# A new order for all five queues of a fused attention and gated-MLP layer

## The chip, the core and the metric

One Trainium2 chip, one of its cores. The metric is the device time of one execution in microseconds (us). Each of the core's five engines works through its own queue in order: PE (matrix products), ACT (activations), DVE (vector work), POOL (vector work) and SP (which here only issues transfers). They meet through semaphores. All transfers run on 16 shared DMA engines.

## The reference

One layer over 2048 positions of width 448, with a modulation computed from a condition vector `c`. A is attention with 16 heads of width 28 and a causal window of 256 positions; B is a gated MLP whose gate mixes positions with a full 2048 x 2048 matrix.

```python
mod = silu(c) @ w_mod                 # six vectors: sa, ca, ga, sb, cb, gb
h = layernorm(x) * (1 + ca) + sa
x = x + ga * A(h, wqkv, wo)           # attention, window 256
h = layernorm(x) * (1 + cb) + sb
x = x + gb * B(h, w_in, w_sp, b_sp, w_out)
# B: z = gelu(h @ w_in); z1, z2 = halves of z; g = w_sp @ layernorm(z2) + b_sp; (z1 * g) @ w_out
```

## The kernel before

The positions are cut into 16 tiles of 128, in four groups of four. Everything stays in the core's own memory between the stages.

- **Loads.** `x_sb` is loaded as tiles 0-1, 2-3, 4-7, 8-11 and 12-15. `w_mod` comes as `wmodA` (the first two vectors, in four pieces, two issued by SP and two by ACT) and `wmodB` (the other four vectors, 1568 KB in one transfer on SP). `wq_st` holds the K and the Q columns of `wqkv` (two pieces each, one on SP and one on ACT), `wv` the V columns. `w_in` comes in three chunks of 448 KB and two halves of 224 KB.
- **First layernorm.** DVE takes the statistics of a tile (L628, L630), POOL the power for the reciprocal root (L632), DVE or POOL writes the normalized tile to `xn` (L643, L650, with L648 for its offset). Group 0 is transposed on PE (L739) and scaled with `modT` on the way out (L748, L750). The other groups are transposed by transfers that SP issues (L465), and then scaled in place (L731). `modT` comes from PE products of `wmodA` (L545) or `wmodB` (L535, with a copied piece `wmodE`, L582); the gates `gg_sb` from L593 and L596.
- **Q, K, V.** L796 makes Q of the first group tile by tile, L762 the Q of later groups, L820 K tile by tile, L840 V.
- **Attention.** For each tile scores (L925 for the first two tiles, L955 and L966 for the rest), exponentials (L911 on ACT), masks (L995, L974 on DVE), products with V (L1002), division (L1016, L1018), a transpose by SP, the output projection (L1028), the residual (L1032) and the second layernorm.
- **The MLP.** L1122 and L1143 make the two halves of z, L1167 mixes positions (28 groups of 16 matmuls, four 512-position blocks `tb` times seven `ft`), L1171 and L1174 form the gated product, L1186 the output product, L1196 the residual. The mixing matrix comes in as 32 transposing transfers, 16 to `wspA` (blocks 0 and 1) and 16 to `wspB` (blocks 2 and 3).

No planner runs in the kernel. The program is a list of numbered operations, and a string `PLAN` says in which order they go out: each word is an engine's letter (p PE, a ACT, d DVE, t POOL, s SP), the operation's number, and after dots the buffer slots that it takes. `Sched.order()` appends the operations to the engines' queues in that order, `count()` and `waits()` work out the semaphore waits from the dependences, and `emit()` writes them out. An operation that several engines can do goes to the engine named by the letter. A word's place in the string matters only against words of the same engine and against users of the same slots.

Numbers that are used below: s14, s1, s10, s12, s13 load x tiles 12-15, 0-1, 2-3, 4-7, 8-11; s20 and s21 the halves of `w_in`'s last chunk, s17 to s19 its other chunks; s2 and s4 `wmodA`; s6 and s8 the K and Q columns; s11 `wv`; s15 `wmodB`; s16 `wo_g`; s193 to s196 are the transposes of x tiles 4 to 7. d186 normalizes tile 4. p45 to p48 are the products of `wmodA`, p125 and p128 the first PE transposes, p93 to p97 the gate products.

Of the kernel before, what the change touches and what calls it, by code (L numbers as in the profile page):

```python
# [22 lines left out]
a403 a43 p421.0 a422.6.0 t249 t253 d404 t251 t199 p375 p379 p381 d406 d382 d399 t252.2 d163 p217.0 p218 a219
a169 p210.1 p211 d212 p429.0 a430.0 p201.0 p202 a203 d168 p204.1 p205 a206 s14 d309 d383.2 p398.0 p400 p448.0
a449.2.1 s16 d426 s831 s258 t254.1 s259 d250.0 d255 d425 d432 d311 s384 s257 t256.3 s260 t100 t99 t261 t102
t262 t264 p226.0 p423.0 a424 p207.1 p227 p405 p208 d228 d305 p407 d408 d409.1 d306 s410 d101 d310 d431 a209
d215 d453 p456.0 p229.0 a457.1 d459 d214 d458 d452 p220.1 p221 p230 a231 p427.0 p428 s833 p475.0 p433 p434
d435 p223.0 p224 d225 d312 p450.0 a222 p232.1 d436.2 s437 d213 a476.3.2 d480 p483.0 d307 p233 d234 p235.0 p236
a451 a216 p477.0 p454.0 p455 a484.0 p501.0 d485 d486 d308 s21 s17 s834 p460 p461 d462 d479 d463.0 s464 a237
t263 p385.0 p386 d387 p411.1 p412 a478 p503.0 d413 t313 a502.6.0 p528.0 a504 d388 d505 d389 p481.0 p482 p487  # L30
p488 p271.0 p530.0 d489 d490.1 a529.2.1 d533 d506 d532 p272 a273 p509.0 a510.5 p268.1 p274.0 p275 d276 p269
d270 p507.0 p508 a531 p555.0 a556.3.2 p281.0 p265.1 p266 a267 d512 p282 p557.0 a558 a283 d511 p513 t317 t318.1
s323 t319 t320.2 s324 d314.0 s321 t315 t316.3 s322 t328 d279 d414 d560 p536.0 a537.1 p438.1 p439 d440 d280
p514 d515 d516.0 p287.0 p288 a289 p290.1 p291 a292 p563.0 a564.5 p238.0 p239 d278 p293.1 p534.0 p294 p535
p582.0 a240 p465.0 p466 d441 d442 d538 d415 d277 s20 s491 s830 s517 t390 d539 d391.2 t392 s393 a295 a583.4.0
d559 p540 p541 p284.1 p584.0 p285 a286 p590.0 a591.2 d566 d467 p299.0 p300 a301 d542 d543.1 p561.0 p562 d586
d565 d468 p567 p568 p608.0 t416 t327 t325 d326 d587 p518.1 p335.0 p519 d569 d570.0 p588.0 a585 p589 p336 d593
d469 d520 a609.3.1 p616.0 d592 d521 d417 d522 t523 t470 t418.0 t524 p338.1 p339 a337 s544 p545.0 p546 s18 p594
p595 a617.5 p635.0 a636.6.2 p610.0 a611 d340 p492.1 p493 d547 p296.0 p297 a298 t471 d596 d597.2 d612 p614.0
d613 s835 s571 s598 d494 t419 s420 d640 d548 d619 d549 d618 d495 t443 t444 t445.1 t446 s447 p662.0 a663.0.0  # L40
d667 p615 p332.0 p333 a334 p329.1 p330 a331 d639 d343 t472.2 d473 s474 p643.0 a644.1 p599.0 p600 p637.0 a638
p345.1 p346 p620 a347 d601 d602 d344 d645 d666 d342 p670.0 a671.2 p621 p664.0 d622 d496 p348.0 p349 a350
p357.1 p358 t550 t551 t552.0 t804 d623.2 s624 p689.0 d646 d673 d525.2 p302.0 p303 d304 d672 s19 p641.0 p642
p647 p648 d649 d805 t553 d650.0 s651 t526 s527 t497 t806 t803 d498.1 t499 s500 a690.5.1 p697.0 a359 p351.1
p352 d341 d353 a665 d693 d603 a698.1 d700 d694 p668.0 p363.0 p364 a365 p715.0 a716.3.2 p669 p674 p675 p691.0
a692 d699 d676 d677.2 s678 p354.1 p355 p572.0 a356 d720 d719 p723.0 a724.2 p717.0 a718 p573 d574 d575 p695.0
p696 p701 d725 p702 d703 d704.0 s705 s554 d576 p652.0 p742.0 a743.0.1 p366.1 p367 a368 d726 p653 d654 t577
d578 t579.2 d746 d655 p721.0 p722 p727 p750.0 a751.4 p728 d747 d729 d730.1 s731 p360.1 p361 p625.0 p744.0 p626
p769.0 d752 d627 d753 d628 a362 p748.0 p679.1 p680 d681 a745 p749 p754 p755 d756 d757.2 p771.0 a770.6.0 p777.0
a772 p706.1 p707 p732.0 p733 d773 d774 p775.0 p776 t580 s581 t809 a778.1 p852.0 p853.1 p854 d656 d708 d734  # L50
d779 d682 d780 d808 t604 d605.0 s758 p759.0 p760 d761 p781 p782 d783 d784.0 a856 d629 t630 t631 p855 a862
p868.3 p869.2 p870 p871 a878 a872 p980.0 p981.1 p982 p983 a986 a987 d735 d736 t657 t658 t606 t659.2 d857 d683
t810 t807 p884.3 p885.2 p886 p887 d709 d710 d632.1 d762 d763 d879 d633 s369 s825 s785 s826 s607 t684 d685 s634
a984 a985 p900.0 p901.1 p902 p903 t737 t711 t660 d686.0 t687 a894 d895 d896 t764 a888 p996.3 p997.2 p998 p999
s661 d712.1 d858 d738 s688 s840 s824 s823 a904 p988.0 d905 a814 a910 p989.1 p990 a1000 a1001 a1003 a992 a1002
a993 p786.0 t799 t797 t713 t811 t813 t801 t812 d765 d889 t766.0 d859 d863 d874 d906 s714 d864 t767 s768 d907
t739.2 d897 d912 t898 d865 d880 d890 p787 d788 d740 s741 s832 p991 a995 d789 d790 t791 d873 d911 d875 t792
d793.1 p932.2 a994 p933.0 p934 p935 a936 d937 p916.1 p917.3 a942 d944 d938 d943 d913 p918 a920 d922 p919 a926
p1004.0 p1005.1 p1006 p1007 a1011 a1009 a1010 a1008 t860 t794 s795 t818 d817 t816 d891 d815 d881 d939 d927
d899 d928 d945 t914 t876 d877 d921 t908 d909 t882 d923 p948.2 p949.3 p950 p951 p964.1 p965.0 p966 a952 d929  # L60
d953 d954 a958 d959 d955 d883 d960 t892 t956 d893 t940 p967 a968 a974 p1028.3 p1029.1 p1030 p1031 t866 t930
t946 t924 t800 a1032 a1033 p1012.2 p1013.3 p1014 a1034 p1020.0 a1035 p1021.1 p1022 p1015 a1017 a1016 a1018
# [5 lines left out]
d1079.0 t1080 t1092 p1045.4 p1039.6 d1046.1 p1153.1 t798 t1047 d1040.0 t1041 d1139.0 p1075.6 p1114.2 p1054.4
p1141.0 p1150.7 d1055.1 t1056 d1076.1 p1060.4 p1147.6 t1077 p1096.5 t1140 d1154.0 p1144.1 d1061.3 d1115.1
p1093.2 d1097.0 t1155 d1145.0 p1102.3 p1063.1 p1057.4 t1146 d1142.0 s1098 d1103.0 t1116 p1105.5 s1062 d1151.1  # L70
d1094.3 t1152 d1058.2 s1059 d1148.1 t1149 d1106.1 t1107 p1069.4 d1070.1 s1071 d1064.1 s1095 s1065 p1108.7
p1117.5 p1111.0 d1109.1 t1110 d1112.1 t1143 p1167.2 p1066.1 t1113 p1163.4 d1118.0 t1119 s1104 d1067.0 s1068
p1168 d1169.0 s1170 p1171.0 p1172 d1173.2 s1174 p1126.3 p1129.6 d1130.0 d1127.1 s1128 s1131 p1159.5 p1160
p1164 d1161.3 s1162 p1099.2 d1165.0 d1100.2 s1101 s1166 p1132.5 d1133.3 s1134 p1135.3 d1136.1 s1137
# [1194 lines left out]
```

## Time and profile before

| | |
|---|---|
| runs | 277.11, 276.43, 281.8 us; median 277.11 |
| the profiled execution | 277.96 us, of which the profile's span is 276.2 us |
| what lies around the span | 1.76 us |
| busy share of the span | PE 97%, PE weight loads 56%, DVE 59%, ACT 44%, POOL 43% |
| chain that ended last, by engine | PE 78%, DVE 13%, DMA 4% |

A line of the chain or of the timeline has its start, its duration, the engine, the tile written and the line of the kernel. "x16" is a count of instructions. A line of a group gives its total busy time and the mean of one in nanoseconds, then the idle time ahead of it and what ended it. A line of the waits gives who waited for whom, the total, the times and the longest. A line of transfers gives the size of one and the median time from issue to landing.

### The profile page before, as it was taken

How to read it: one execution, taken by the hardware profiler on the slowest of the kernel's cores; microseconds unless marked ns; L12 is line 12 of the kernel's file. 1: busy time of each engine (PE TensorE's matmuls, PEld its weight loads, DVE VectorE, ACT ScalarE, POOL GpSimd, SP SyncE). 2: the span in 40 equal slices, each digit the busy share in tenths (PEclk: the TensorE clock that was granted, in tenths of full speed). 3: DMA queues.
4: the chain of work that ended last, by engine and by line, in shares of the span. 5: the costliest groups of instructions: out<-in, count | busy, mean ns of one | idle time of the engine just before them, and what ended most of it. 6: DMA issues, size and time to landing. Idle time of an engine off the chain costs nothing.

```text
span 276.2 us, 8403 instructions
## 1 busy us (share of the span) xinstructions
PE 268.5 (97%) x3751; PEld 155.1 (56%) x3751; DVE 163.7 (59%) x365; ACT 121.5 (44%) x142; POOL 118.1 (43%) x160
## 2 busy tenths in 40 slices
PE   7999998999999899999999999999999999999995
PEld 5976686678677676544444444444444444454552
DVE  3799999979899989939789301221212022153143
ACT  2599998899899689476766500000000000000000
POOL 7565467626574231498258003254453023062320
PEclk9999999999999799999999999999999999999999
DMA  7999744845442533658499996000000000001013
GB/s 206 316 221 189 96 101 114 107 96 110 114 63 61 107 60 61 176 114 141 97 155 191 213 182 135 0 0 0 2 0 0 0 2 0 33 17 63 0 39 116
DMA packets 67301, 25.54 MB, mean 92 GB/s; under 512 B 58497, under 2 KB 66178, under 8 KB 67266
## 3 DMA queue, kind: packets, MB, share of 16 engines
q1 hardware_dynamic: 66304, 24.21, 43.8%
q10 hardware_dynamic: 962, 0.80, 1.1%
q8 instruction: 29, 0.48, 0.8%
q14 instruction: 6, 0.05, 0.1%
HBM read 9.01 MB, written 1.84 MB: 39 GB/s over the span
## 4 chain that ended last, share of the span: by engine, by line
PE 78%; DVE 13%; DMA 4%; POOL 1%; SPq 1%; issue 1%; DVEq 0%
PE ps L1167 35%; PE ps L1122 8%; PE ps L1143 8%; PE ps L1186 8%; PE ps L1002 5%; DVE PT L974 4%; PE ps L1028 4%; PE ps L955 3%; DMA x_sb<-in_A_x_dram 3%; PE ps L820 3%; PE ps L762 2%; DVE st_all L628 2%; PE ps L840 2%; DMA hT<-xn 2%; DVE o_sb L1018 1%
## 5 line engine op out<-in xcount | busy, mean ns | idle before, releaser
L1174 POOL TENSOR_TENSOR z1T<-tmpg,z1T 128x512 bf16<-128x512 bf16 x28 | 32.0, 1153 | 77.2 <-DVE tmpg L1171 77.2
L1171 DVE TENSOR_TENSOR tmpg<-ps,bsp_bc 128x512 bf16<-128x512 f32 x28 | 19.0, 689 | 76.0 <-PE ps L1167 64.7
L911 ACT ACTIVATE PW<-ps 128x2048 bf16<-128x2048 f32 (+1 forms) x42 | 59.9, 1451 | 6.1 <-PE ps L955 4.5
L1167 PE MATMUL ps<-wspB,z 128*128 128x512 bf16 x224 | 50.1, 379 | 0.0
L1167 PE MATMUL ps<-wspA,z 128*128 128x512 bf16 x224 | 49.5, 379 | 0.0
L632 POOL TENSOR_TENSOR rs_all<-mv_all,neghalf 128x1 f32<-128x1 f32 (+2 forms) x37 | 24.1, 672 | 34.3 <-DVE mv_all L630 34.3
L974 DVE TENSOR_TENSOR PT<-PW,mask 128x1024 bf16<-128x1024 bf16 x56 | 38.0, 702 | 0.2
L1167 PEld LDWEIGHTS ps<-wspA,z 128*128 128x128 bf16 x224 | 21.8, 98 | 26.6 <-issue 0.4
L1167 PEld LDWEIGHTS ps<-wspB,z 128*128 128x128 bf16 x224 | 21.9, 98 | 26.2
L1002 PE MATMUL ps<-Vaug,PT 128*128 128x32 bf16 x496 | 23.3, 177 | 1.4 <-DVE o_sb L1018 1.4
L1002 PEld LDWEIGHTS ps<-Vaug,PT 128*128 128x128 bf16 x496 | 21.4, 96 | 4.3 <-DVE o_sb L1018 2.2
L1122 PE MATMUL ps<-w_in,hT 64*128 64x448 bf16 x224 | 22.0, 350 | 0.0
L1186 PE MATMUL ps<-w_out_g,z1T 128*128 128x448 bf16 (+2 forms) x119 | 22.0, 342 | 0.0
L1143 PE MATMUL ps<-hT,w_in 64*128 64x512 bf16 x196 | 22.0, 376 | 0.0
L628 DVE BATCH_NORM_STATS2 st_all<-z 128x6 f32<-128x448 bf16 x32 | 18.4, 606 | 5.8 <-ACT z L1129 5.8
L628 DVE BATCH_NORM_STATS2 st_all<-x_sb 128x6 f32<-128x448 bf16 x32 | 19.4, 615 | 2.9 <-DMA x_sb<-in_A_x_dram 2.7
L1002 PE MATMUL ps<-Vaug,PW 128*128 128x32 bf16 x224 | 19.7, 177 | 0.0
L820 PE MATMUL ps<-hT,WQK 112*128 112x128 bf16 x256 | 17.9, 223 | 1.6 <-DVE KT L833 1.1
L1151 ACT ACTIVATE z1T<-ps 128x512 bf16<-128x512 f32 x28 | 14.6, 603 | 9.1 <-PE ps L1143 9.1
L1196 DVE TENSOR_TENSOR fin<-ps,x_sb 128x448 bf16<-128x448 f32 (+2 forms) x17 | 9.8, 595 | 14.7 <-PE ps L1186 9.9
L1002 PEld LDWEIGHTS ps<-Vaug,PW 128*128 128x128 bf16 x224 | 17.6, 96 | 1.1
L1129 ACT ACTIVATE z<-ps 128x896 bf16<-128x896 f32 x16 | 13.9, 913 | 7.9 <-PE ps L1122 5.4
(105 smaller groups left out, 354.1 us busy)
## 6 DMA issues: line engine op xcount, KB each, us to landing
out_dram<-fin SPq DMA_DIRECT2D x15, 112.0 KB, 1.7
wmodB<-in_w_mod_dram SPq DMA_DIRECT2D x1, 1568.0 KB, 15.0
x_sb<-in_A_x_dram SPq DMA_DIRECT2D x3, 448.0 KB, 8.0
w_in<-in_B_w_in_dram SPq DMA_DIRECT2D x3, 448.0 KB, 4.5
w_out_g<-in_B_w_out_dram SPq DMA_DIRECT2D x1, 784.0 KB, 4.7
bsp_bc<-in_B_b_sp_dram SPq DMA_DIRECT2D x1, 512.0 KB, 5.1
x_sb<-in_A_x_dram SPq DMA_DIRECT2D x2, 224.0 KB, 4.8
hT<-xn SPq DMA_TRANSPOSE x28, 3.2
```

Source lines behind the costliest of these rows:

```text
L628: st = [dve(0.62, lambda e, t=t, o=12 - 6 * (n - ci), s=s: e.bn_stats(st_all[:, slot, t, o:o + 6], s()), deps(t), prio) for ci, s in enume ...
L632: return pool(0.4 + 0.15 * len(tiles), lambda e: e.tensor_tensor(rs_all[:, slot, a:b], mv_all[:, slot, a:b, 1], neghalf[:, 0:b - a], ALU.pow),
L820: km = lambda g, kc, start, stop, h=h, t=t: lambda e: e.matmul(ps[:, h.slot[0], g * 128:(g + 1) * 128], lhsT=WQK[0:CP, kc, 16 + 4 * g:20 + ...
L911: ex = act(xdur, lambda e, out_ap=out_ap, in_ap=in_ap: e.activation(out_ap(), in_ap(), ACT.Exp, scale=SCALE), [s] + list(after), v - 8.0 + ...
L974: return lock_d(0.68, lambda e: e.tensor_tensor(cols(hp.slot[0] * 2048 + 1024 * k, [[256, 4], [128, 2], [1, 128]]), cols(at_w() + pad + at ...
L1002: fns.append(lambda e, hp=hp, hO=hO, hi=hi, bi=bi, kb=kb, hd=hd, nb=nb, a=at[hi][bi], p_of=p_of: e.matmul(ps[:, hO.slot[0], 32 * hd:32 * h ...
L1122: return lambda e, kc, p0, start, stop: e.matmul(ps[:, hs[t % 2].slot[hf], 0:D], lhsT=hT[p0:p0 + 64, kc, t * 128:(t + 1) * 128], rhs=w_in[ ...
L1143: return lambda e, kc, p0, start, stop: e.matmul(ps[:, hs[b // 2].slot[b % 2], :], lhsT=w_in[p0:p0 + 64, kc, ft * 128:(ft + 1) * 128], rhs ...
L1167: m = pe(16 * MMS, [lambda e, h=h, si=si, ft=ft, tb=tb: e.matmul(ps[:, h.slot[0], :], lhsT=z2[:, si, ft * 128:(ft + 1) * 128], rhs=(wspA i ...
L1171: a = dve(0.7, lambda e, h=h, ht=ht, tb=tb: e.tensor_tensor(tmpg[:, ht.slot[0], :], ps[:, h.slot[0], :], bsp_bc[:, tb * 512:(tb + 1) * 512 ...
L1174: u = pool(1.16, lambda e, ht=ht, ft=ft, tb=tb: e.tensor_tensor(z1T[tb][:, ft, :], tmpg[:, ht.slot[0], :], z1T[tb][:, ft, :], ALU.mult), [ ...
L1186: return [lambda e, ft=ft: e.matmul(ps[:, h.slot[0], 0:hi - lo], lhsT=z1T[t // 4][:, ft, (t % 4) * 128:(t % 4 + 1) * 128], rhs=w_out_g[:, ...
```

## The change

Only the string `PLAN` changes; every operation, its shape and its dependences stay. All five queues get a new order, and 70 operations change their engine (37 come to DVE and 27 leave it; the rest moves between ACT and POOL).

- SP's queue before: s1 s2 s4 s6 s10 s8 s12 s13 s11 s15, the four transposes s193 to s196, s14 s16. After: s14 s21 s20 s1 s2 s4 s6 s10 s18 s19 s8 s12 s16 s13 s11, the transposes s195 s194 s196 s193, then s15.
- The `wmodA` products p45 to p48 stood together ahead of the transposes p125 and p128. Now: p45, p46, then p125, then p47, p48, then p128.
- V products (p143, p152) stand ahead of the Q and K products of tiles 2 and 3.
- In the position mixing, the first group that reads `wspB` (p1123) is the fourth group; before it was the eighth.

```diff
 PLAN = """
-d24 d22 p50.1 p59.3 p51.2 p58.0 p60.1 p62.0 a0 a3 a5 a7 a9 d23 d25 d26 d27 p40.1 p68.2 p74.3 p64.1 p52.0 p67.2
-p53.3 p76.0 p49.3 p70.0 s1 s2 s4 d113 s6 s10 s8 a41 p45.0 p46 p47.1 p48 p73.2 p75.1 p63.2 t30 t31 t32 t35 t36
...
-d123.0 p134.3 p131.6 p69.3 p56.0 p146.0 p147 p61.2 a132 d177 d184 d135 a136 s13 d243 d179 d178 d182 d180 t28
-t185 t191 t187 t189 d245 d44 d241 d186.3 s11 p143.7 p370.0 a133 p164.1 p171.6 p172 d244 p165 d166 a148 p152.0
...
-d246 d167 d374 p158.7 p159 a160 s15 p93.1 p94 d95 d248 d87 d88 d242 d397 p96.0 p97 d98 d378 s193 t188.1 s194
...
-d867 s828 s822 s827 s829 s820 s844 s821 s851 s845 s850 t972 d973 d957 t962 d963 p1087.4 p1051.5 s819 p1036.1
...
+s14 t33 t30 d27 d22 d23 d24 p57.2 p49.1 t31 a0 a3 p40.1 p78.2 p68.0 p75.3 p62.2 p77.0 s21 s20 a5 a7 a9 a41 t34
+t36 t32 s1 p70.2 p55.3 p66.2 d26 p54.1 t35 d25 d113 p58.1 p51.1 p61.1 d111 d114 d112 s2 t115 p67.1 p69.2 s4
+p72.3 p74.2 t37 d116.0 p45.1 p60.3 p65.3 d117.2 s6 p46 p125.2 a106 p47.0 d85 p48 p128.7 d105 p84.2 p83.2 p76.2
+d86 a126 p64.3 d129 p81.1 p71.1 p59.3 s10 s18 t39 t110 t28 d104 d130 d103 p79.1 p52.2 d118 p50.1 p82.2 p63.3
+s19 p73.2 s8 s12 d120 p80.1 d119 d107 s16 a127 d121 d179 s13 t122 a109 d181 p149.6 p150 p140.1 p141 a108
+d124.1 a151 a42 d123.2 p146.7 s11 p137.3 p147 d183 d180 d177 a142 p138 a148 d182 d184 p56.2 p134.0 a139 d178
+p131.6 t38 p53.2 a135 a132 p370.0 d136 t185 p143.7 a371.6 t187 d133 p152.0 p164.6 p144 p165 p155.1 d245 a145
+a166 d189 d246 d190.2 p376.0 t188.1 t191 d241 p156 p171.6 p172 a377.1 d243 d247 a157 d311 s195 d374 d372
+p394.0 p158.7 d248 d186.3 d378 d44 s194 t29 t192.0 p153 a173 p373.0 s196 d242 d244 a395.2 d168 s193 d154 p375
+d170 d380 p159 s15 p93.1 p94 a396 d87 p96.0 a160 d95 d397 p401.0 t249 p97 a402.6 a403 d255 d169 d98 d167 t88
...
 """
```

More of the change, by code (lines that the diff above doesn't have):

```diff
@@ L23 @@
[L23 to L62, printed above, removed]
@@ L68 @@
[L68 to L72, printed above, removed]
@@ new lines @@
+p271.0 p481.0 a529.6.1 p530.0 p482 s17 s323 s321 s437 p487 p488 p272 d413 d388 a531 p509.0 t315 p557.0 p268.1
+d506 d389 a273 a510.2 t316.3 p274.0 p269 p275 d489 d490.2 d414 a270 d505 d532 p507.0 d512 d276 p555.0 p265.1
+d415 p266 p281.0 t416 a556.4.2 d267 d511 d533 p282 a558 p508 p438.1 p536.0 p439 a283 p287.0 p513 d440 p514
+p288 d559 d417 d515 a537.5 a278 d280 p290.1 d516.1 p291 s324 s464 d277 d292 p563.0 d441 t390 a289 a279 s829
+s322 d560 d539 d391.1 t325 d538 p238.0 p534.0 s491 s832 p293.1 s517 p239 p294 a564.2 d442 a295 p535 t443
@@ new lines @@
+p637.0 d618 d619 p333 s598 s831 a638 d495 d331 a334 p643.0 p345.1 p615 d473 p346 p620 d548 p621 p599.0 a644.5
+p670.0 d496 d639 d342 d622 d640 d549 a347 a341 a671.6 d623.2 d645 d646 p357.1 p664.0 p641.0 p600 p358 p642
+s474 t523 p689.0 d601 t804 t524 t550 p348.0 a665 s624 a359 t551 d672 p647 p302.1 d666 d667 a690.3.1 p303
+t525.0 t805 p648 p349 d344 t526 d304 a350 p697.0 p351.1 p352 p363.0 d649 d694 d693 d650.1 p668.0 d353 a698.2
+p364 a343 d673 p715.0 a716.4.2 t497 p669 p691.0 d365 p572.0 p573 p674 d699 d602 d700 p675 a692 p354.1 d676
@@ L75 @@
+d1109.1 d1145.0 d1103.1 p1069.1 p1150.2 p1141.4 p1147.5 t1110 t1146 d1151.1 d1142.0 d1070.3 t1152 t1143
+p1111.2 d1148.1 t1149 p1167.4 p1163.0 p1168 p1164 s1104 s1071 p1114.3 p1171.6 p1172 d1112.0 d1169.1 d1173.3
+d1165.2 s1166 d1115.1 p1105.1 t1113 t1116 p1159.0 d1106.0 p1160 p1099.3 d1161.2 s1170 d1100.1 s1162 t1107
+p1126.7 p1132.5 d1127.2 s1128 s1101 s1174 d1133.0 p1129.0 d1130.2 s1134 s1131 p1135.5 d1136.1 s1137
 """
```

49 lines of the change are left out of this document (38 added, 11 removed).

## The prediction

> **What bounds the kernel now.** I read the page first, then the chain that ended last in order of time, then the waits, then the early stretches one by one. The page gives the frame.
>
> ```profile
> span 276.2 us, 8403 instructions
> PE 268.5 (97%) x3751; PEld 155.1 (56%) x3751; DVE 163.7 (59%) x365; ACT 121.5 (44%) x142; POOL 118.1 (43%) x160
> ```
>
> PE is called busy for 97%, but the ends of matmuls are modelled, so that figure hides small gaps. What PE really waits for stands in the chain and in PE's own waits.
>
> ```profile
> 3.91 7.49 DMA x_sb<-in_A_x_dram
> ...
> 19.79 1.22 SPq L465
> 21.05 4.35 DMA hT<-xn
> ...
> 27.28 0.07 DVE modT L554
> ...
> 27.49 1.05 PE ps L820 x16
> 28.55 0.88 PE ps L762 x4
> ...
> 155.13 76.08 PE ps L1167 x352
> ```
>
> ```profile
> PE ps L1002 <- DVE o_sb L1018: 1.4, 1, 1.4
> PE ps L820 <- DVE KT L833: 1.1, 1, 1.1
> ```
>
> Up to 27.5 us the chain runs through loads: the second group of x lands at 11.40, four transposes of its normalized tiles land at 25.40, and the second half of the modulation products (DVE's modT at L554) releases the first K and Q products of x tiles 4 to 7 at 27.49. They end at 29.43. From there PE waits only twice for over a microsecond. So whatever makes 27.49 later has little on PE to be won back from, and the question is what the new order does before that point.
>
> **The start: what the loads cost.** SP issues its loads in order, and in this trace they also land in order, each later the more stands ahead of it.
>
> ```profile
> x_sb<-in_A_x_dram SPq DMA_DIRECT2D x2, 224.0 KB, 4.8
> wmodA<-in_w_mod_dram SPq DMA_DIRECT2D x2, 196.0 KB, 4.4
> wq_st<-in_A_wqkv_dram SPq DMA_DIRECT2D x2, 196.0 KB, 6.4
> x_sb<-in_A_x_dram SPq DMA_DIRECT2D x3, 448.0 KB, 8.0
> wv<-in_A_wqkv_dram SPq DMA_DIRECT2D x1, 392.0 KB, 9.2
> wmodB<-in_w_mod_dram SPq DMA_DIRECT2D x1, 1568.0 KB, 15.0
> w_in<-in_B_w_in_dram SPq DMA_DIRECT2D x3, 448.0 KB, 4.5
> w_in<-in_B_w_in_dram SPq DMA_DIRECT2D x2, 224.0 KB, 3.8
> wo_g<-in_A_wo_dram SPq DMA_DIRECT2D x1, 392.0 KB, 5.7
> w_out_g<-in_B_w_out_dram SPq DMA_DIRECT2D x1, 784.0 KB, 4.7
> wmodA<-in_w_mod_dram ACTq DMA_DIRECT2D x2, 196.0 KB, 4.1
> ```
>
> wmodA and wq_st have the same 196 KB, but 4.4 and 6.4 us; 448 KB take 8.0 in the crowd and 4.5 alone (w_in). The stretches show why (the last column is GB/s, the one before it the DMA engines' busy share): the transfers are at their rate from 2 us on.
>
> ```profile
> 2.00:6.00 4.00, 3.86 (x25) 2.55 (x24) 1.53 (x5) 1.46 (x2) 3.26 (x6) 1.00 1.01 284
> 6.00:10.00 4.00, 3.71 (x48) 3.17 (x46) 2.44 (x8) 1.62 (x3) 2.53 (x7) 1.00 1.10 293
> 10.00:14.00 4.00, 3.94 (x63) 3.79 (x64) 3.75 (x11) 2.33 (x5) 1.84 (x4) 1.00 1.11 334
> 14.00:18.00 4.00, 4.00 (x64) 3.25 (x62) 3.52 (x12) 3.97 (x6) 2.40 (x6) 1.00 1.03 285
> ```
>
> That is 1.14 MB by 6 us, 2.31 by 10, 3.64 by 14 and 4.78 by 18. The second x group has 2464 KB up to its own end (1680 on SP, 784 in ACT's four loads of 196), 2.52 MB, which the curve reaches at 10.6; it landed at 11.40. I take 1.0 us of lag after the curve.
>
> The new SP queue begins with x tiles 12 to 15 (448 KB) and both halves of w_in's last chunk (448 KB), which nobody needs for long; only then come x tiles 0 and 1, wmodA, wq_st's K columns and x tiles 2 and 3. Then two more w_in chunks (896 KB), wq_st's Q columns, x tiles 4 to 7, wo_g, x tiles 8 to 11, wv. Landing times, SP's bytes plus ACT's 784 KB:
> - x tiles 0 and 1: 1.15 MB on SP, 1.95 with ACT's. By the curve 8.8 + 1.0 = 9.8 us (7.0 if ACT's loads took nothing; ACT's row shows that they take their part, so 9.8).
> - x tiles 4 to 7: 4256 KB = 4.36 MB: 16.5 + 1.0 = 17.5, against 11.40 before.
> - x tiles 8 to 11: 5.22 MB, at 285 GB/s beyond 18 us: 20.5. wv: 5.62 MB: 21.9. So "V ahead" of the late Q and K puts products at a place in PE's queue where their weights are not there: PE stands at the first V product until 21.9.
>
> **The late one: wmodB behind the transposes.** Before, wmodB was issued at once and landed at 6.20 + 15.0 = 21.2.
>
> ```profile
> 6.20 2.23 SPq L393 DMA_DIRECT2D wmodB<-in_w_mod_dram  x1
> ```
>
> Now it stands in SP's queue behind the four transposes of x tiles 4 to 7. The last of these waits for DVE's norm d186, and DVE's new queue has d186 behind the statistics of x tiles 8 to 11 and one of tile 15. DVE's durations:
>
> ```profile
> L628 DVE BATCH_NORM_STATS2 st_all<-x_sb 128x6 f32<-128x448 bf16 x32 | 19.4, 615 | 2.9 <-DMA x_sb<-in_A_x_dram 2.7
> L630 DVE BATCH_NORM_AGGREGATE mv_all<-st_all 128x2 f32<-128x9 f32 x32 | 5.7, 184 | 0.3
> L643 DVE TENSOR_SCALAR xn<-x_sb,mv_all,rs_all 128x448 bf16<-128x448 bf16 x11 | 4.2, 394 | 0.8 <-POOL rs_all L632 0.8
> L650 DVE TENSOR_SCALAR xn<-x_sb,rs_all,nm_all 128x448 bf16<-128x448 bf16 x4 | 1.9, 470 | 0.0
> L648 DVE TENSOR_SCALAR nm_all<-mv_all,rs_all 128x1 f32<-128x1 f32 x6 | 1.2, 203 | 0.5 <-POOL rs_all L632 0.5
> L750 DVE TENSOR_SCALAR hT<-ps,modT 112x256 bf16<-112x256 bf16 x3 | 1.2, 404 | 0.0
> L995 DVE TENSOR_TENSOR PT<-PT,mask 128x512 bf16<-128x512 bf16 x8 | 3.0, 399 | 0.0
> ```
>
> From 17.5: four statistics 2.46, two norms 0.79, four aggregates 0.74, two hT writes 0.81: 22.3, past the landing of x tiles 8 to 11. Then five statistics 3.08, two aggregates 0.37, nm 0.20, one norm of each form 0.86, two masks 0.80: d186 ends at 27.6. The transpose's issue takes 1.22 (the row at 19.79), so wmodB is issued at 28.8. Its price alone: 784 KB took 4.7 (w_out_g); the other 784 KB (0.80 MB) at 285 GB/s is 2.8, together 7.5; at least 7.1 at the best stretch's 334 GB/s, at most 7.5 plus the 4.35 of a transpose ahead of it. I take 7.5, nearest to w_out_g's row: wmodB lands at **36.3**, 15.1 later than before.
>
> On PE and DVE everything stands behind it. PE's queue has the gate products (L593) ahead of the rest, DVE's has the wmodE copy (L582). PE has done before that point what it had done before at 21.4 (64 K and 64 Q matmuls at L820 and L796, eight V, 32 scores), give or take eight small ones: nothing is gained. After the landing:
>
> ```profile
> L593 PE MATMUL ps<-wmodB,sc_rep 112*128 112x448 bf16 x8 | 1.7, 352 | 0.0
> 23.81 0.60 DVE L596 COPY gg_sb<-ps 128x448 f32<-128x448 f32 x1
> 25.43 1.12 DVE L731 TENSOR_SCALAR hT<-hT,modT 112x512 bf16<-112x512 bf16 x2 [0.68 <-DMA hT<-xn]
> ```
>
> Eight L593 matmuls with a score group between them, 2.0; the second gg copy with what is before it on DVE, 0.9; 32 small products at L535, 1.1; then modT and two L731, which the new queue puts behind modT, 1.4. The first product of tiles 4 to 7 starts 5.5 us after the landing, at 41.8, and that group ends (0.88 + 1.05) at 43.7 instead of 29.43: **14.3 us late**. The transposes themselves no longer count there: they land about 33.
>
> The modulation products in three parts around the transposes (L545, L739) cost nothing by themselves: they wait for wmodA and x, which now land about 10; the DVE and PE work there has only loads to wait for.
>
> **What comes back.** PE's waits after 29.43 are 1.4 + 1.1, and after the first of them its clock was low:
>
> ```profile
> 27.50:110.00 82.50, 80.06 (x2348) 58.76 (x2348) 77.81 (x164) 72.76 (x71) 39.01 (x47) 0.98 0.50 91
> 90.90:95.00 4.10, 4.05 (x115) 3.60 (x116) 3.81 (x9) 1.82 (x2) 0.33 (x2) 0.59 0.38 89
> ```
>
> 4.1 us at 0.59 lose at most 1.7, so 4.2 us in all can be recovered. Against it: 37 operations move to DVE and 27 leave it, by their rows some 4 us more in a stretch where DVE has 4.7 us free (82.5 less 77.81), and PE's new wait ahead of L593 can bring its own 1.7 of low clock (an estimate from the landings: wv at 21.9, then about as much work as PE had before between wv and wmodB, some 7 us, so that PE stands from 29 to 36). I take 0.3 for the balance. The sum: 277.96 + 14.3 - 0.3 = 292.0 in a profiled execution; the median of the runs shown is 277.11, 0.85 lower, so **291**.
>
> The Trainium skill (TensorE: Matmul & The Clock Gate, Part 1: The HAM clock gate) says that an idle window of about 3.4 us halves the clock until as long a busy one. By that rule the new wait costs 1.7, the same as the row's price; but the row shows 0.59 after a wait of 1.4 only, and here the measurement decides.
> The Trainium skill (DMA: Bandwidth & Descriptors, Anatomy of one DMA) fits 2.0 us + bytes / 436 GB/s, for DMAs issued from GpSimd. An estimate from that page for wmodB is 5.7 us; the sum would then be 290.2. The w_out_g row (4.7 us, where the fit gives 3.8) speaks for the longer one.
>
> **Rivals.**
> 1. The loads in front do not delay the others, because the engines share queued transfers. Then x lands as before (11.40), DVE's list gives 11.4 + 4.8 + 5.3 = 21.5 for d186, wmodB is issued at 22.7 and lands at 30.2: 9.0 late, 8.2 at the end of the first group of tiles 4 to 7. With all 4.2 won back the time is 282.0, as a median 281.1: not slower by 2%. The rising landing times above speak against it. It decides if x tiles 0 and 1 land before 5 us. Chance 0.11.
> 2. The end adds a wait. L1167's fourth group, no longer its eighth, reads wspB. A group takes 76.08 / 22 = 3.46, so wspB is due 10.4 after the first group instead of 24.2. Before, SP's last eleven went at 1.53 each:
>
> ```profile
> 151.91 16.84 SPq L465 DMA_TRANSPOSE wspB<-in_B_w_sp_dram  x11
> ```
>
>    They were all issued at 168.75; now 22 instead of 26 wsp transposes stand behind the last attention tile, 6.1 less, so 162.6 + some 4 of landing against 165.5 due: 1 us of wait, and up to 4 if the norm's transposes between them wait. With DVE's 4 us on top: 294 to 298. Chance 0.20.
> 3. The change does what it says and V, Q and K fill PE's early time: it would have to end the products of tiles 4 to 7 before 29.43, with wmodB at 21.2 or sooner. The queue speaks against it. Time 272 to 277; chance 0.03.
>
> **The numbers.** The forecast has 0.66, the others as given. A measurement of this kernel tells about 2% (5.5 us) from no change. Slower by over 2% (above 282.7): forecast and rival 2 whole, half of rival 1: 0.92. Within 2%: the other half, and a little of rival 3: 0.06. Faster by over 2%: 0.02. The range for 8 in 10: down to 284 (x tiles 4 to 7 at 334 GB/s throughout, 1.4 sooner; DVE's 26 listed instructions overlapping by 0.05 each, 1.2; wmodB 0.4 sooner; 4.2 won back instead of 0.3), up to 298 (rival 2, wmodB behind a transpose).
>
> **What would show it.** Right: x tiles 0 and 1 land at 7 to 10 us, wmodB is issued after 25 and lands after 33, PE has one wait of 5 us or more ending at L593, the first L762 starts about 42, and everything from the first L1122 on is shifted by about 14. Wrong: wmodB landing before 30, or a first L762 before 36; then the time can't be above 286. A wait at the fourth L1167 group would show rival 2.

## The result, and the profile after

The changed kernel takes 300.02 us (median of 4 runs, 299.1 to 301.49) against 278.0 for the kernel before on the same chip: a ratio of 1.0818, 95% interval 1.0727 to 1.0908. The forecast of 291 (284 to 298) had the sign and the first cause right and was 9 us short. The profiled execution took 301.49 us. (Medians below are over all runs of a kernel; ratios and their intervals leave out runs that a low clock disturbed.)

The page of the changed kernel: the span, the busy shares, and the granted clock in 40 slices of 7.5 us.

```profile
span 299.8 us, 8399 instructions
PE 274.1 (91%) x3740; PEld 158.0 (53%) x3751; DVE 166.2 (55%) x375; ACT 125.2 (42%) x147; POOL 110.9 (37%) x145
PEclk9699759999999999799999999999999999999999
```

PE's share fell from 97% to 91%, and its clock is low in three places: near 10, from 30 to 45, and at 120. PE's longest waits (total, times, longest) say what stands ahead of each:

```profile
PE ps L593 <- DMA wmodB<-in_w_mod_dram: 10.5, 1, 10.5
PE ps L545 <- DMA wmodA<-in_w_mod_dram: 4.8, 1, 4.8
PE ps L1028 <- DVE x_sb L1032: 1.7, 1, 1.7
PE ps L564 <- DVE st_all L488: 1.2, 1, 1.2
PE ps L1122 <- DVE st_all L628: 1.1, 1, 1.1
```

The chain that ended last, around the longest of them (start, duration, what):

```profile
27.64 0.27 DVE xn L643
...
30.38 0.88 SPq L465
...
31.31 8.21 DMA wmodB<-in_w_mod_dram
...
39.56 2.42 PE ps L593 x6
...
42.53 0.86 PE ps L593 x2
...
44.77 1.01 PE ps L535 x32
...
45.96 1.60 DVE hT L731 x2
...
47.70 0.59 PE ps L762 x2
48.29 0.89 PE ps L820 x16
49.19 0.43 PE ps L762 x2
```

SP's own timeline shows why wmodB is issued at 31.31 and not right after DVE's norm at 27.91: the four transposes ahead of it, the first released at 24.80, keep SP busy for 6.47 us without a gap.

```profile
24.80 6.47 SPq L465 DMA_TRANSPOSE hT<-xn  x4
31.31 0.58 SPq L393 DMA_DIRECT2D wmodB<-in_w_mod_dram  x1
```

The stretch around the wait and the first work after it (busy times of PE, weight loads, DVE, ACT and POOL, then the granted clock, the DMA engines' busy share and GB/s), and the rows of the mixing products (shortest, median and longest in ns, then the first and the last start in us):

```profile
33.00:43.00 10.00, 3.44 (x24) 1.37 (x25) 1.99 (x5) 0.42 (x1) 1.75 (x2) 0.53 0.53 154
40.00:44.00 4.00, 4.00 (x27) 1.55 (x26) 2.48 (x5) 1.39 (x2) 2.32 (x4) 0.53 0.00 0
```

```profile
L1167 PEld LDWEIGHTS ps<-wspA,z x224: 96/98/99, 178.6 to 233.5; 128*128 128x128 bf16 x112
L1167 PEld LDWEIGHTS ps<-wspB,z x224: 97/98/98, 188.8 to 288.2; 128*128 128x128 bf16 x112
```

So the execution splits into three parts at points that both orders have: the start, up to the end of the first K and Q products of tiles 4 to 7 (1.92 after the first L762 in the new order; the old order takes them the other way round); the middle, up to the first weight load of L1167; and the tail. Before: 29.4, 125.7, 121.1. After: 49.6, 129.0, 121.2. The start lost 20.2, the middle 3.3, the tail 0.1.

One chain of the middle shows its kind of loss: a norm waits for a transpose that still reads its buffer, the residual behind it on DVE is late, and PE stands 1.7 us and then works at a low clock (0.79 from 120 to 128; the last fence is the stretch, its columns as above).

```profile
116.35 4.28 DMA hT<-xn
...
120.66 0.40 DVE xn L643
...
122.31 0.93 PE ps L1028 x2
```

```profile
120.00:128.00 8.00, 6.31 (x160) 3.72 (x158) 6.07 (x14) 4.54 (x5) 4.02 (x6) 0.79 0.32 68
```

### The profile page after: what moved, and what is told of

Read it like the earlier page. It is cut to its first block, busy times and chain, and to the rows that moved or that the text cites. A ratio compares the mean times of both kernels' runs of the same rounds, so it can differ in the third digit from the quotient of the medians.

```text
span 299.8 us, 8399 instructions
## 1 busy us (share of the span) xinstructions
PE 274.1 (91%) x3740; PEld 158.0 (53%) x3751; DVE 166.2 (55%) x375; ACT 125.2 (42%) x147; POOL 110.9 (37%) x145
## 4 chain that ended last, share of the span: by engine, by line
PE 74%; DVE 12%; DMA 8%; ACT 2%; issue 1%; SPq 1%; POOL 0%
PE ps L1167 32%; PE ps L1186 7%; PE ps L1143 6%; PE ps L1122 5%; DVE PT L974 4%; PE ps L1002 4%; PE ps L762 4%; PE ps L955 3%; PE ps L1028 3%; DMA hT<-xn 3%; DMA wmodB<-in_w_mod_dram 3%; PE ps L820 3%; DMA wmodA<-in_w_mod_dram 3%; PE ps L840 2%; DVE st_all L628 2%
## 5 line engine op out<-in xcount | busy, mean ns | idle before, releaser
L1174 POOL TENSOR_TENSOR z1T<-tmpg,z1T 128x512 bf16<-128x512 bf16 x28 | 31.9, 1152 | 82.2 <-DVE tmpg L1171 82.2
L1171 DVE TENSOR_TENSOR tmpg<-ps,bsp_bc 128x512 bf16<-128x512 f32 x28 | 19.2, 690 | 70.2 <-PE ps L1167 66.6
L1167 PE MATMUL ps<-wspB,z 128*128 128x512 bf16 x218 | 49.3, 379 | 0.3
L1167 PE MATMUL ps<-wspA,z 128*128 128x512 bf16 x219 | 48.4, 379 | 0.4 <-issue 0.2
L632 POOL TENSOR_TENSOR rs_all<-mv_all,neghalf 128x1 f32<-128x1 f32 (+2 forms) x37 | 25.5, 702 | 51.2 <-DVE mv_all L630 51.1
L1167 PEld LDWEIGHTS ps<-wspA,z 128*128 128x128 bf16 x224 | 21.8, 98 | 26.6 <-issue 0.4
L1167 PEld LDWEIGHTS ps<-wspB,z 128*128 128x128 bf16 x224 | 21.9, 98 | 25.7
L1002 PE MATMUL ps<-Vaug,PT 128*128 128x32 bf16 x496 | 24.9, 177 | 0.6 <-DVE o_sb L1018 0.6
L1002 PEld LDWEIGHTS ps<-Vaug,PT 128*128 128x128 bf16 x496 | 22.8, 96 | 4.8 <-DVE o_sb L1018 1.5
L1122 PE MATMUL ps<-w_in,hT 64*128 64x448 bf16 x224 | 22.7, 349 | 1.3 <-DVE st_all L628 1.1
L628 DVE BATCH_NORM_STATS2 st_all<-x_sb 128x6 f32<-128x448 bf16 x32 | 18.8, 608 | 8.6 <-DMA x_sb<-in_A_x_dram 8.6
L1143 PE MATMUL ps<-hT,w_in 64*128 64x512 bf16 x196 | 22.9, 376 | 0.0
L1002 PE MATMUL ps<-Vaug,PW 128*128 128x32 bf16 x224 | 20.6, 177 | 0.0
L1028 PE MATMUL ps<-wo_g,hT 112*128 112x448 bf16 x64 | 16.5, 366 | 1.7 <-DVE x_sb L1032 1.7
```

The costliest lines, as they stand in the source:

```text
L628: st = [dve(0.62, lambda e, t=t, o=12 - 6 * (n - ci), s=s: e.bn_stats(st_all[:, slot, t, o:o + 6], s()), deps(t), prio) for ci, s in enume ...
L632: return pool(0.4 + 0.15 * len(tiles), lambda e: e.tensor_tensor(rs_all[:, slot, a:b], mv_all[:, slot, a:b, 1], neghalf[:, 0:b - a], ALU.pow),
L1002: fns.append(lambda e, hp=hp, hO=hO, hi=hi, bi=bi, kb=kb, hd=hd, nb=nb, a=at[hi][bi], p_of=p_of: e.matmul(ps[:, hO.slot[0], 32 * hd:32 * h ...
L1028: mo = pe2(4 * MMD, [lambda e, h=h, j=j, ch=ch: e.matmul(ps[:, h.slot[0], 0:D], lhsT=hT[0:CP, ch, j * 128:(j + 1) * 128], rhs=wo_g[0:CP, c ...
L1122: return lambda e, kc, p0, start, stop: e.matmul(ps[:, hs[t % 2].slot[hf], 0:D], lhsT=hT[p0:p0 + 64, kc, t * 128:(t + 1) * 128], rhs=w_in[ ...
L1143: return lambda e, kc, p0, start, stop: e.matmul(ps[:, hs[b // 2].slot[b % 2], :], lhsT=w_in[p0:p0 + 64, kc, ft * 128:(ft + 1) * 128], rhs ...
```

## Experiments: the start

Three kernels take the new order and put loads back: wmodB alone, the other loads alone, and both. Two do the reverse to the kernel before.

**wmodB alone.** s15 goes from behind the transposes to behind s11.

```diff
-SP: ... s13 s11 s195 s194 s196 s193 s15
+SP: ... s13 s11 s15 s195 s194 s196 s193
```

> The new order with one word moved: wmodB's load (s15) is issued ahead of the four transposes of x tiles 4 to 7, right behind wv; the five early loads stay in front. Theory (the wait for wmodB is most of the loss): wmodB is issued about 14 us, lands about 27 (5.5 us after wv, which landed about 21), the wait of 10.5 us ahead of L593 falls to under 1, the last transpose lands about 34.5 and the first L762 starts about 37 instead of 47.7: 10.7 us less, a time of 289 to 291. Rival (PE would wait for something else there, or the rest of the new order is what costs): less than 4 us less, above 296.

Measured 291.02 us, ratio 1.0482 (1.0408 to 1.0556). wmodB was issued at 14.10, PE did not wait for it, and the first L762 came at 36.26 instead of 47.70. With the other loads still in front, the place of wmodB is 9.0 of the 22 us.

**The other loads alone.** x tiles 12 to 15 and three chunks of w_in go back behind what is needed first; wmodB stays behind the transposes.

```diff
-SP: s14 s21 s20 s1 s2 s4 s6 s10 s18 s19 s8 s12 s16 s13 s11 s195 s194 s196 s193 s15
+SP: s1 s2 s4 s6 s10 s8 s12 s16 s13 s11 s14 s195 s194 s196 s193 s15 s21 s20 s18 s19
```

> The new order with the five early loads moved back on SP's queue: x tiles 12 to 15 behind wv, the four w_in loads behind wmodB; wmodB stays behind the transposes. Theory (loads are served in the order of issue): x tiles 0 and 1 land at 3.6 instead of 9.9, x tiles 4 to 7 at about 11.5, the first transpose is issued about 18.5 and the fourth about 24, wmodB is issued at 25 instead of 31.3 and lands at 33, the first L762 starts about 41.4: 6.3 us less, 293 to 295. Rival (queued loads share the engines, so that their order means little): x tiles 0 and 1 land late as well and the time stays above 298.

Measured 294.91 us, ratio 1.0567 (1.0492 to 1.0642): 5.1 less. wmodB was still waited for, 7.1 us.

**Both.** The load of wo_g (s16) moves too, behind wmodB.

```diff
+SP: s1 s2 s4 s6 s10 s8 s12 s13 s11 s14 s15 s16 s195 s194 s196 s193 s21 s20 s18 s19
```

> The new order on PE, ACT, DVE and POOL with a repaired start of SP's queue: small loads first, x tiles 12 to 15 behind wv, then wmodB and wo_g ahead of the transposes, the w_in loads behind them. Theory (the start costs 20 of the 23.5 us, the later part of the new order costs 3 to 4): wmodB lands at 23, the last transpose about 28.5, the first L762 starts about 31, and the time is 281 to 285, still above the kernel before. Rival (the order behind the start is as good or better, and the late 3 to 4 us came from the shift): 274 to 279.

Measured 283.63 us, ratio 1.0189 (1.0146 to 1.0233): 16.4 of the 22 are back. That is 2.3 more than the sum of each alone (14.1), which is no more than the spread of these medians: in the traces the first L762 came 11.4 sooner with wmodB alone, 7.5 with the other loads alone and 18.5 with both, so the two add up. The products of tiles 4 to 7 ended at 31.2, where the old order has 29.4, and the middle took 129.3: of what is left, 1.7 lie in the start and 3.6 in the middle.

**wmodB late in the kernel before**, one word of SP's queue moved.

```diff
-SP: ... s11 s15 s193 s194 s195 s196 s14 s16
+SP: ... s11 s193 s194 s195 s196 s15 s14 s16
```

> The kernel before with one word moved: wmodB's load is issued behind the four transposes of x tiles 4 to 7; nothing else. Theory: it is issued at 23.2 instead of 6.2 and lands about 31.4 instead of 21.2, PE stands about 9 us ahead of L593 and then runs at a low clock for some 4 us, and the first L820 of x tiles 4 to 7 starts at 37.5 to 39.5 instead of 27.5: 288 to 290. Rival (the transposes land sooner without wmodB beside them and pay it back): below 283.

Measured 291.76 us, ratio 1.0474 (1.0427 to 1.0522). SP's timeline and PE's wait:

```profile
19.25 6.51 SPq L465 DMA_TRANSPOSE hT<-xn  x4
25.80 0.58 SPq L393 DMA_DIRECT2D wmodB<-in_w_mod_dram  x1
```

```profile
PE ps L593 <- DMA wmodB<-in_w_mod_dram: 10.6, 1, 10.6
```

The wait of 10.6 us and SP's 6.5 us appear in the old order too: that one word makes them, without the rest of the new order. The time is a little above what was expected, for the reason that the prediction has too (SP's time for four transposes was counted as one). The middle took 124.6: it isn't lengthened by a late start as such.

**The loads in front in the kernel before.**

```diff
-SP: s1 s2 s4 s6 s10 s8 s12 ...
+SP: s14 s21 s20 s1 s2 s4 s6 s10 s18 s19 s8 s12 ...
```

> The kernel before, with the loads of x tiles 12 to 15 and of both halves of w_in's last chunk put ahead of all others on SP, and two more chunks of w_in ahead of the Q columns, as in the new order; all else as before. Theory: x tiles 0 and 1 land near 9.5, tiles 4 to 7 near 17, and the first products of tiles 4 to 7 end 5 to 7.5 later: 283 to 286. Rival: the new order's own early queues are at fault, and the old order has slack for late loads: under 281.

Measured 284.62 us, ratio 1.0215 (1.0163 to 1.0266), as the theory said. PE's longest wait was now for wmodA, and the middle took 126.3.

```profile
PE ps L545 <- DMA wmodA<-in_w_mod_dram: 6.4, 1, 6.4
```

**Is PE's clock part of the start?** The changed kernel with 88 matmuls of the filler tile ahead of the first gate product.

```diff
-PE: ... p159 p93.1 p94 ...
+PE: ... p159 p1175.0 p93.1 p94 ...    # 88 matmuls, fill x fill, into a bank that p96 overwrites
```

> The changed kernel, with 88 matmuls of the filler tile put on PE ahead of the first gate product, where PE waits 10.5 us for wmodB; they write a bank that the second gate product overwrites. Theory: the eight gate products took 3.3 us instead of 1.7 and what follows was slow because PE's clock was low after the wait; with fillers the gate products take 1.7, the first group of tiles 4 to 7 ends 1.5 to 2.5 us sooner: 297.5 to 299. Rival: DVE's steps (copies of the gates, modT, scaling) set that stretch: 299.5 to 301.

```profile
29.73 9.78 PE L1206 MATMUL ps<-fill 128*128 128x256 bf16 x88 [0.27 <-DVE Vaug L845]
40.05 1.31 PE L593 MATMUL ps<-wmodB,sc_rep 112*128 112x448 bf16 x6 [0.53 <-DMA wmodB<-in_w_mod_dram]
```

The first six gate products took 1.31 instead of 2.42, and from the first of them to the first L762 it was 6.0 us instead of 8.1: the clock cost 2.1 there. The total, 299.65 us, ratio 1.0658 (1.0569 to 1.0747), overlaps the changed kernel's. (The profiled execution was the longest of the four, so its middle of 130.5 says little.) So the gain in the stretch is shown, a gain of the total is not.

## Experiments: the middle

The base is the new order with both loading faults mended (283.63 us, middle 129.3). The question is why its middle takes 3.6 us more than the old order's 125.7.

**A fourth xn2 buffer.** The norms of the second layernorm take four buffers in turn.

```diff
-xn2, xn2_off, _ = alloc("xn2", [128, 3, DP], BF16)
+xn2, xn2_off, _ = alloc("xn2", [128, 4, DP], BF16)
-x2R = Res(range(3), ...)
+x2R = Res(range(4), ...)
```

> The new order with both loading faults mended (283.63 us), and a fourth buffer for the normalized tiles of the second layernorm (xn2), taken in turn. The middle, from the end of the first products of tiles 4 to 7 to the first mixing product, took 129.6 there against 125.7 in the kernel before. Theory A: DVE's norms wait for the transposes that hold the three buffers, everything of the end of the attention queues behind them on DVE; with the fourth buffer those waits go and half of the 3.9 or more comes back: 281 to 282.2. Theory B: the waits are a symptom, the order of PE and DVE sets the pace: 283 to 284.2, middle 129 or more.

Measured 284.03 us, ratio 1.0144 (1.0085 to 1.0202), overlapping that of the base. The wait at L1028 was gone, but one of 2.1 us at L1122 came, behind a scaling (L1053) that waited for one of the last transposed tiles:

```profile
138.02 4.88 DMA hT<-xn
...
142.93 0.41 DVE hT L1053
```

The middle was still 129.2. SP's timeline points to why those tiles land late: it issues almost without a gap, with wspA and wspB between the transposes of the second layernorm (hT<-xn).

```profile
121.18 2.65 SPq L465 DMA_TRANSPOSE wspB<-in_B_w_sp_dram  x2
123.87 1.30 SPq L465 DMA_TRANSPOSE wspA<-in_B_w_sp_dram  x1
125.22 4.49 SPq L465 DMA_TRANSPOSE hT<-xn  x3
129.76 1.29 SPq L465 DMA_TRANSPOSE wspB<-in_B_w_sp_dram  x1
131.09 1.30 SPq L465 DMA_TRANSPOSE wspA<-in_B_w_sp_dram  x1
132.43 1.30 SPq L465 DMA_TRANSPOSE wspB<-in_B_w_sp_dram  x1
133.77 2.58 SPq L465 DMA_TRANSPOSE hT<-xn  x2
136.80 1.17 SPq L465 DMA_TRANSPOSE wspB<-in_B_w_sp_dram  x1
138.02 1.26 SPq L465 DMA_TRANSPOSE hT<-xn  x1
```

**Five wspB transposes later, three buffers.**

```diff
-SP: ... s785 s844 s845 s826 ... s741 s842 s825 s847 s714 s768 s849 s795 ... s820 ...
+SP: ... s785 s826 ... s741 s825 s714 s768 s795 ... s820 s844 s845 s842 s847 s849 ...
```

> The new order with both loading faults mended (283.63 us), and five transposes of the second half of the mixing matrix (wspB), which stood among the last transposes of attention and second layernorm, moved behind the last one of the first half. Theory A: the transposes of attention and norm are slowed and queued behind those of the mixing matrix (hT from o_sb lands 3.7 us after its issue, 2.5 in the kernel before); moved away, 1 to 3 of the middle's 3.9 come back: 280.5 to 282.6. Theory B: those waits lie beside other work: 283 to 284.2. If the end then waits for wspB at the fourth group of mixing products, the tail is over 121.5.

Measured 289.0 us, ratio 1.0243 (1.0153 to 1.0332): no gain. In the profiled execution, the longest of the six, the wait at L1028 behind the norms' three buffers was still there (1.8 us), and one of 4.1 us appeared at L1167: the load of the bias (bsp_bc) had slid back in SP's queue. The bias hides what the transposes did, so it tells little.

**Four buffers, and the scaling that held up DVE moved six places back.**

```diff
-DVE: ... d937 d817 d945 d921 d912 d913 d922 d927 ...
+DVE: ... d937 d945 d921 d912 d913 d922 d927 d817 ...
```

> The new order with both loading faults mended and four xn2 buffers (284.03 us; undisturbed about 282.9), and one more word moved: DVE's scaling of the last transposed group (L1053, third chunk) five places later, behind statistics of z that it held up. With four buffers alone PE had no more wait at L1028, but one of 2.1 us at L1122 (for the statistics behind that L1053, which waited 2.8 for a transpose), and its clock was low for some 4 us after it. Theory: each such wait costs its length and 1.7 of low clock; without it 3.8 come back, 279 to 280.5, and the middle takes 125 to 126.5 as in the old order. Rival: the new order's PE queue is slower by itself by small stalls; then less than half comes back: 281.5 to 283.

Measured 285.27 us, ratio 1.029 (1.024 to 1.0341): worse. PE now waited for the scaling itself, so the tile was late in earnest and DVE's order was not the cause.

```profile
PE ps L1122 <- DVE hT L1053: 3.5, 1, 3.5
```

**The same with x tiles 12 to 15 loaded behind the transposes.**

```diff
-SP: ... s11 s14 s15 s16 s195 ...     DVE: ... d247 d311 d374 ...
+SP: ... s11 s15 s16 s195 s194 s196 s193 s14 ...     DVE: ... d306 ... d311 d312 ...
```

> The same, and x tiles 12 to 15 loaded behind the four transposes, as in the kernel before, with the statistics of tile 15 moved to those of tiles 12 and 13. wmodB then has 448 KB less ahead of it. Theory: PE's wait of 1.2 for wmodB goes, the first products of tiles 4 to 7 end 1 to 1.8 us sooner, and the time is 277.5 to 279.2. Rival: DVE's list up to the last norm of tiles 4 to 7 sets the start, not wmodB; then no more than 0.5 better than the other run.

Measured 289.11 us, ratio 1.0356 (1.0291 to 1.0422). The first L762 came at 29.57, 0.5 earlier, as the rival said; PE waited 4.0 at L1122 and the clock was low twice. It shows only that the start did not hang on wmodB any more; why the total is longer was not followed up.

**Four buffers and five wspB transposes later**: the two edits above together, the scaling in its old place.

> The new order with both loading faults mended and four xn2 buffers (284.03 us; undisturbed about 282.9), the scaling in its old place, and five transposes of wspB moved from among the last transposes of attention to behind the last of wspA. In the run with four buffers SP issued without a gap from 104 to 148 us, five wspB and six wspA among the attention's, and PE's only longer wait of the middle (2.1 us at L1122, 1.7 more at a low clock) ended with the last transposed tile at 142.9. Theory: SP's queue sets that wait; five times 1.3 less ahead of it, it lands 3 to 6 sooner: 280 to 281.5, the middle 125.5 to 127. Rival: the transposes wait for DVE's norms, not for SP; then 282.5 to 285.

Measured 285.96 us, ratio 1.0289 (1.0239 to 1.0338), but the profile shows the theory's point: the first mixing product came at 155.7 instead of 160.7, so that the middle took 124.8, and what it gained was lost at once in the tail.

```profile
L1167 PEld LDWEIGHTS ps<-wspA,z x224: 96/98/152, 155.7 to 215.4; 128*128 128x128 bf16 x112
```

```profile
159.66 5.28 DMA bsp_bc<-in_B_b_sp_dram
...
165.04 0.70 DVE tmpg L1171
...
165.79 5.75 PE ps L1167 x18
```

The bias load stands behind the moved transposes on SP; the first L1171 waits for it and PE for the bank.

**Five of wspA later as well**, and all of wspB behind wspA.

```diff
-SP: ... s731 s821 s581 s758 s828 s369 s822 s661 s607 s785 s826 ... s741 s825 s714 s768 s795 s823 ...
+SP: ... s731 s581 s758 s369 s661 s607 s785 ... s741 s714 s768 s795 s821 s828 s822 s826 s825 s823 ...
```

> The same with five more, those of wspA, moved behind the attention's last transpose, and all of wspB behind wspA. Theory: nothing but attention's own transposes is left in front, and the time is at least as good as with five moved: 279.5 to 281.5. If the first mixing product then waits for the last wspA, a wait at L1167 shows it and its length is the loss. Rival as before: 282.5 to 285.

Measured 293.9 us, ratio 1.051 (1.0453 to 1.0568). The wait foreseen at L1167 came, 10.8 us long, but for the bias, issued at 169.56 behind most of the mixing matrix, and not for wspA. The middle was no shorter than with wspB alone moved (127.3 against 124.8).

**The bias ahead of the moved transposes**, with four buffers, with three, and (four buffers) in the changed kernel with its late loads.

```diff
-SP: ... s820 s844 s845 s842 s847 s849 s837 s841 s819 ...
+SP: ... s820 s819 s844 s845 s842 s847 s849 s837 s841 ...
```

> The new order with both loading faults mended, four xn2 buffers, five wspB transposes behind the last of wspA, and the load of the bias (bsp_bc) ahead of these five. Theory: the first mixing product stays near 155.7, the bias lands before it is needed, the tail is 121 again: 277.5 to 279.5, no slower than the kernel before. Rival: the clock or another transfer takes the place of the bias: 282 or more.

> The same with the three xn2 buffers of both kernels. Theory: SP's queue is the larger part, and with transposes that land sooner the three buffers hold less: 278.5 to 281.5. Rival: the three buffers alone cost the middle's 4 us, because norms wait for them whatever SP does: 282.5 to 284.5.

> The changed kernel with its late loads as they are, and only the middle's remedies: four xn2 buffers, five wspB transposes behind the last of wspA, the bias load ahead of them. Theory: the start stays (first products of tiles 4 to 7 end near 49.6), the middle takes 125 to 127 instead of 129.2: 296 to 298.5. Rival: in this kernel the shifted start hides the middle's waits, and nothing comes back: 299.5 to 302.

| kernel | us | ratio (95%) | first L762 | middle | tail |
|---|---|---|---|---|---|
| four buffers | 286.85 | 1.0289 (1.0246 to 1.0333) | 29.16 | 125.1 | 127.9 |
| three buffers | 289.84 | 1.0404 (1.0354 to 1.0454) | 31.30 | 128.6 | 128.4 |
| changed kernel | 304.64 | 1.0931 (1.0875 to 1.0987) | 46.11 | 126.1 | 130.2 |

The middle came back with four buffers, in both starts, and hardly with three, where PE still waited 1.6 us at L1028: SP's order and the buffers have to change together. But the totals got worse by another wait, at the fourth mixing group (four buffers):

```profile
PE ps L1167 <- DMA wspB<-in_B_w_sp_dram: 4.2, 1, 4.2
```

This is the wait that the prediction's second rival foresaw. In the changed kernel itself it does not appear: five transposes of wspB are issued early, among the last ones of the second layernorm, and the price is paid there instead.

**The two mixing groups that read wspB moved back**, from the fourth and sixth place to the eighth and ninth, in both starts.

```diff
-PE: p1042 p1048 p1087 p1123 p1081 p1156 p1051 p1036 p1072 p1084 ...
+PE: p1042 p1048 p1087 p1081 p1051 p1036 p1072 p1123 p1156 p1084 ...
```

The additions (L1171) and gatings (L1174) of the two groups move along on DVE and POOL.

> The run with both loading faults mended, four buffers, five wspB transposes behind wspA and the bias ahead of them (286.85 us), and the two mixing groups that read wspB moved from the fourth and sixth place to the eighth and ninth. Theory: no wait for wspB, first mixing product near 156, tail 121: 278 to 280, the same as the kernel before within 1%. Rival: another wait of the end takes its place: 283 or more.

> The changed kernel with its late loads, four buffers, five wspB transposes behind wspA and the bias ahead of them (304.64 us), and the same two mixing groups moved to the eighth and ninth place. Theory: first mixing product near 174, tail 121: 296 to 298, that is 3 to 4 less than the changed kernel (300.02). Rival: the end waits all the same: 300 or more.

Measured 280.79 us, ratio 1.0048 (0.9997 to 1.0098), and 296.69 us, ratio 1.0673 (1.0604 to 1.0742). With everything mended the new order is as fast as the old one within 1%. It still has the new engines of the 70 operations, the early V products and the split wmodA products, so these together, gains and losses, cost no more than that. With its late loads kept it is 3.3 below the changed kernel, within what was expected, though those two intervals overlap by a little.

**The last 1.6 us of the start**: DVE's norms of tiles 7 and 4 ahead of the statistics of tiles 8 to 11 and 15, L731 ahead of modT.

```diff
-DVE: ... d133 d245 d189 d246 d190 d241 ... d248 d186 ... d199 d176 d92 d197 d200 ...
+DVE: ... d133 d189 d190 d186 d245 d246 d241 ... d248 ... d199 d197 d200 d176 d92 ...
```

> The run with loads, buffers, SP's order and mixing groups mended (280.79 us; undisturbed near 279.0), with DVE's norms of tiles 7 and 4 ahead of the statistics of tiles 8 to 11 and 15, and the scalings of the transposed tiles 4 to 7 (L731) together ahead of modT. Theory: the last of the four transposes is released 3 us sooner, lands 1 to 1.5 sooner because SP needs 1.3 for each of the four, and the first products of tiles 4 to 7 end near 29.8: 277.5 to 279. Rival: the gate products behind wmodB set the start, and nothing is won: 279 to 281.

Measured 280.56 us, ratio 1.0092 (1.0042 to 1.0141): nothing won. The transposes landed at 27.5, no sooner than before (27.3), and the scalings moved ahead now held up modT; the first group ended at 32.25. Its profile gives the middle and the tail of the mended order:

```profile
31.82 0.43 PE ps L762 x2
```

```profile
L1167 PEld LDWEIGHTS ps<-wspA,z x224: 96/98/99, 157.2 to 212.0; 128*128 128x128 bf16 x112
```

From 32.25 to 157.2 are 125.0, and its span of 278.3 leaves 121.1. No version was found that beats the kernel before.

## Why the prediction was wrong, step by step

The path was right up to wmodB. Four terms of the sum failed, all to the same side: SP's issue of wmodB, its landing, the stretch from there to the first products of tiles 4 to 7, and the middle.

**Right.** The loads: x tiles 0 and 1 were to land at 9.8, and DVE's first statistics began at 9.91. d186 was to end at 27.6 and ended at 27.91. wmodB behind the transposes, one wait of PE over 5 us ending at L593 and no wait at the fourth L1167 group in the forecast case: all as written. (The first L762, about 42 by the forecast, came at 47.70.) The cause of most of the loss, 16.4 of 22 us, was named, and the experiments split it as 9.0 for wmodB's place and 5.1 for the loads in front, with 2.3 within the spread. The first rival (loads that don't delay each other) and the third (a gain) are out: x tiles 0 and 1 landed twice as late as its 5 us, and no kernel with the new order was faster than the one before.

**The issue of wmodB, 28.8; measured 31.31.** The step "The transpose's issue takes 1.22 (the row at 19.79), so wmodB is issued at 28.8" counted the last transpose alone. SP needs 6.47 for the four, so that the first, released at 24.8, set the time and not the last. The row to read was in the timeline of the kernel before, too:

```profile
17.10 6.13 SPq L465 DMA_TRANSPOSE hT<-xn  x4
```

**The landing, 7.5 after issue; measured 8.21.** 0.7 short; in the old order behind the transposes it was 8.5. The Trainium skill (DMA: Bandwidth & Descriptors, Anatomy of one DMA) gives 5.7 as an estimate. The measurements of this transfer issued late, 8.2 to 9.6, are further from that than from the 7.5 worked out from the w_out_g row.

**From landing to the first L762, 5.5; measured 8.2.** The eight gate products with the score group between them were put at 2.0 and took 3.83, at a clock of 0.53; the fillers brought the stretch from the landing down to 6.1. (The four parts in the prediction add up to 5.4, not 5.5.) The clock stood in the sum once, with 1.7 in "what comes back", but as something that could offset a gain, not as a term here. The Trainium skill (TensorE: Matmul & The Clock Gate, Part 1: The HAM clock gate) has the clock halved after an idle window of some 3.4 us until as long a busy one; the 0.53 after a wait of 10.5 agrees with that. The low clock after waits of 1.7 to 2.1 us in the middle is not covered by that sentence; these runs show it all the same.

**The middle, 0.3 won; measured 3.3 lost.** This is the term that failed in kind. I costed DVE's 4 us of added work and PE's clock, and took SP's queue into account only for the end, in rival 2: there I counted how many wsp transposes stand behind the last attention tile (22 instead of 26), and not where they stand among the transposes of the second layernorm. The runs showed two causes in a row. With three xn2 buffers, the norms wait for transposes that still read them, and PE stands 1.6 to 1.7 us at L1028. With a fourth buffer PE stands 2.1 us at L1122 instead, for a tile whose transpose SP issues in between those of wspA and wspB. Only both remedies together brought the middle from 129.3 to 125.1; the buffer alone gave 129.2, SP's order alone 128.6. The four wsp transposes more that stand before the last attention tile were not shown to cost anything: with three of them moved back as well, the middle was 127.3. DVE's added work is out as the cause, since it was all still there at 125.1. Once five of wspB had been moved back, wspB came 4.2 to 6.0 us late for the fourth group. So rival 2 had the right transfers in the wrong place: the new group order demands wspB sooner, and SP pays for it in the middle.

**The sum.** 2.5 for SP's issue, 0.7 landing, 2.7 after it, 3.6 in the middle (3.3 lost, 0.3 not won): 9.5, and 292.0 + 9.5 is the profiled 301.5. Of the 2.7, the clock is 2.1 by the run with fillers.

**Open.** How the remaining 0.5% (-0.03% to 1.0%) of the mended order against the old one comes about was not settled; its start ends some 1.6 us later, and moving the norms did not change that. Why the new order needs a fourth buffer where the old one does with three was not settled either.

## What to carry to other kernels

When a plan moves a step behind others on an issuing queue, add up the issue times of all that stand ahead of it, from the moment when the first of them is released, and not only the last one's. When a consumer is moved forward (here the mixing groups that read wspB), its transfers are pulled forward too, and the cost shows where they squeeze in, not where the data is used. A wait that is removed is proved harmless or costly only when the one that takes its place is looked up in the next profile: buffers, bias, wspB and group order had to change together before the time moved.

## What was not expected of the hardware

- One DMA transpose of a 128 x 512 tile holds SP's queue for 1.2 to 2.8 us, median 1.27, and four in a row for 5.2 to 6.6 us in the first six traces of the start; loads behind them start only after that.
- After a wait of PE of 1.7 us in the middle the granted clock was 0.79 over 8 us; 0.21 of 8 us is 1.7, an estimate that it costs as much again as the wait. After 10.5 us it was 0.53 over the 4 us of work behind the wait, and 88 small matmuls into a spare bank during it brought the six gate products from 2.42 to 1.31 us.
- The same 1568 KB transfer took 15.0 us when issued early beside others and 8.2 us when issued late, with nothing behind it on SP until it had landed; issued early it is still the one that lands in time.
